# Row norms and down-weight sums moved from GpSimd to VectorE and spread over the loop, with another order of row blocks and loads

## The chip, the cores and the metric

The kernel runs on one core of a Trainium2 chip. The metric is the device time of one execution in microseconds (us), taken as the median of several runs. A core has five engines, each with its own queue of instructions: TensorE (PE, matrix products), VectorE (DVE), ScalarE (ACT), GpSimd (POOL) and SyncE (SP), which here issues most of the DMAs. An engine works through its queue in order, and a wait for a semaphore holds everything behind it.

## What is computed

```python
def reference(A_x, A_k_cache, A_v_cache, A_wq, A_wo, B_x, B_W_gate, B_W_up, B_W_down):
    x = A_x                                   # 1 x 2048 x 512, bfloat16
    xn = _layernorm(x, axis=-1)
    s = _A_ref(xn, A_k_cache, A_v_cache, A_wq, A_wo)   # q = xn @ wq, 32 heads of 128,
                                              # softmax(q k^T / sqrt(128)) v over 2048 keys, @ wo
    g = _silu(_B_ref(xn, B_W_gate, B_W_up, B_W_down))  # (relu(xn Wg) * (xn Wu)) @ Wd, F = 1792
    return x + s * g
```

## The kernel before, in words

The 2048 rows are worked in four row blocks of 512 (Q = 0 to 3), each of four tiles of 128 rows (n = 4Q to 4Q+3). The 32 heads are in eight groups of four. The main loop runs over 1024 *positions*: a block of the loop is one head with one row block, and has eight positions; each position makes the scores of 256 keys (`emit_S_tile`, L1481, three positions ahead), the exponential on ACT (L1493) and the product with V (`emit_PV_tile`, L1590). At the end of a block `emit_norm_block` divides by the row sums on DVE (L1510, L1513) and turns the result by DMA on SP's queue (L1518). The first eight blocks alternate between heads 0 and 1 (`hq_of`), so that a row block is used twice before the next is needed.

All other work is put at positions by hand, at the end of the function: `put(P, ...)` places products on PE, `aside(P, ...)` places work of the other engines at position P of the first blocks. What is placed at a position is issued after its scores and ahead of its product with V. What bears on the change:

- The layer norm. `front` makes the first four row tiles one by one ahead of the loop: statistics and aggregate on DVE (L398, L404), a square root on ACT (L407), the reciprocal on DVE, the norm itself on DVE for tile 0 and on POOL for tiles 1 to 3 (`ln_norm`, L431), a transpose on PE. PE then projects four heads of row block 0 (`head_q`, L503), whose results go out of PSUM by `q_out` (L513 on ACT, L515 on DVE). Row blocks 1, 2, 3 follow in `front`: four statistics, four aggregates and a chain of twelve small DVE instructions for the reciprocal square root (`ln_coef`, L419 to L425), then four norms on POOL, then four DMA transposes on SP into `xnT` (`ln_rows_turn`, L449; for block 3 at position 8).
- The plain projections, `emit_qplain` (L758): a head's queries of one row block from `xnT`, placed at positions 8, 10, 20, 24 and later.
- `emit_tx` (L581 to L589): four DVE sums over row blocks 0 and 2, later over 1 and 3, which the gated products need. Products are made in Strassen's manner: seven products (m = 1 to 7) of sums of blocks in place of eight.
- The gated unit, `emit_gu` (from GU0 = position 13, a step at each position; from GU1 = 67 for the other two row blocks). The 1792 columns are worked in chunks of 128, two chunks in seven steps, each step with two products (`gu_prod`, L1037) in one pair of PSUM banks. `gu_out` takes each to SBUF, most on DVE (a copy L1051, sums L1052), one on ACT (L1060). A product of the next step may add into a bank that this step's DVE instruction has to copy first. The lower rows' multiply is on POOL (L1073), the upper rows' on DVE (`gu_hi`, L1081), issued in the step of its product m = 3.
- `gu_prep`: a chunk's weights W are scaled (L605 on ACT; for chunks 0 and 1 L607 on POOL) and four sums SG made on POOL (L612 to L617).
- The down product (`emit_d`, L1129): its weight is loaded at position 20 (L651), scaled on DVE at 25 and 28 (L657), and its four sums of 128x1792 are made on POOL at positions 30, 36, 42, 48 (`emit_wd_sums`, L668 to L674). `emit_hs` makes sums of the gated unit's result on DVE. `emit_sw` scales a part of Wq on POOL (L635) and makes four sums there.

## Time and profile before

| | |
|---|---|
| median of 3 runs | 1301.07 us (1300.12 to 1302.04) |
| the profiled execution | 1303.03 us, its span 1301.6 us |
| PE busy | 1250.4 us (96%) |
| ACT busy | 1049.4 us (81%) |
| DVE busy | 929.2 us (71%) |
| POOL busy | 778.6 us (60%) |
| mean granted clock of TensorE | 0.990 |

In a row of the timeline stand the start and the duration in us, the engine, the line, the operation, out<-in, size and count, and in brackets how long the engine was idle ahead of it and what ended that. A row of groups has `xcount | busy, mean ns | idle before`. A row of a stretch has the time of each engine in it, then the granted clock, the DMA's share and GB/s.

### The profile page before, as it was taken

What the parts mean: (1) busy time and instruction counts of PE and PEld (TensorE: products, weight loads), DVE (VectorE), ACT (ScalarE), POOL (GpSimd) and SP (SyncE); (2) the same over time, 40 slices, a digit from 0 to 9 for tenths busy, and PEclk for the clock granted to TensorE, in tenths of its full rate; (3) what the DMA queues carried; (4) which work ended last, traced back from release to release, by engine and by line L of the source; (5) the groups of instructions that cost most, each with busy time, mean ns of one, the idle gap of its engine ahead of it and who ended that gap; (6) DMA issues with size and microseconds to landing.
All of it is one profiled execution on the core that took longest, in us unless ns stands there. A gap on an engine that the chain in (4) does not pass through costs nothing.

```text
span 1301.6 us, 29330 instructions
## 1 busy us (share of the span) xinstructions
PE 1250.4 (96%) x11957; PEld 819.3 (63%) x11957; DVE 929.2 (71%) x1389; ACT 1049.4 (81%) x1114; POOL 778.6 (60%) x879
## 2 busy tenths in 40 slices
...
GB/s 186 49 106 38 72 47 33 82 38 42 116 56 50 50 62 66 50 50 65 58 45 40 56 58 55 50 46 74 58 49 50 66 65 47 50 66 111 134 34 134
DMA packets 287396, 84.73 MB, mean 65 GB/s; under 512 B 265504, under 2 KB 287264, under 8 KB 287264
## 3 DMA queue, kind: packets, MB, share of 16 engines
...
## 4 chain that ended last, share of the span: by engine, by line
PE 80%; DVE 3%; issue 1%; ACT 0%; DVEq 0%; ACTq 0%
PE ps_acc L1590 33%; PE ps_r L1481 31%; PE ps_r L920 5%; PE ps_r L1320 3%; PE ps_r L1380 2%; PE ps_r L1037 2%; PE ps_r L1129 2%; PE ps_r L1622 1%; PE ps_r L787 1%; DVE g_sb L1159 1%; PE ps_r L1411 1%; PE ps_r L1412 0%; DVE uB L1052 0%; ACT PT L1493 0%; PE ps_r L1703 0%
## 5 line engine op out<-in xcount | busy, mean ns | idle before, releaser
L1493 ACT ACTIVATE PT<-ps_r 128x1024 bf16<-128x1024 f32 x1024 | 993.3, 1028 | 211.9 <-PE ps_r L1481 200.3
L1590 PEld LDWEIGHTS ps_acc<-V_sb,PT 128*128 128x128 bf16 x8192 | 544.3, 98 | 238.2 <-issue 36.8
L1590 PE MATMUL ps_acc<-V_sb,PT 128*128 128x129 bf16 x8192 | 629.1, 221 | 4.4 <-DVE Onorm L1513 3.4
L1481 PE MATMUL ps_r<-QT_sb,KT_sb 128*128 128x512 bf16 x2048 | 601.5, 381 | 9.8 <-ACT PT L1493 3.0
L925 DVE TENSOR_TENSOR UVR<-UVR,ps_r 128x512 f32<-128x512 f32 (+1 forms) x228 | 168.7, 755 | 85.2 <-PE ps_r L920 83.1
L1481 PEld LDWEIGHTS ps_r<-QT_sb,KT_sb 128*128 128x128 bf16 x2048 | 159.9, 98 | 37.4 <-DVE UVR L925 4.3
L1290 DVE TENSOR_TENSOR s_acc<-s_acc,ps_r 128x1024 f32<-128x1024 f32 x130 | 156.8, 1219 | 32.6 <-PE ps_r L1320 22.5
L885 POOL TENSOR_TENSOR TI<-xn_sb 128x512 f16<-128x512 f16 x48 | 55.9, 1165 | 96.8 <-PE ps_r L920 96.8
L1298 DVE TENSOR_TENSOR s_acc<-s_acc,ps_r 128x512 f32<-128x512 f32 x116 | 77.4, 686 | 22.1 <-PE ps_r L1380 17.9
L1513 DVE TENSOR_TENSOR Onorm<-ps_acc,rz_sb 128x512 bf16<-128x512 f32 x127 | 87.8, 692 | 4.4
L925 DVE TENSOR_TENSOR QT_sb<-UVR,ps_r 128x512 bf16<-128x512 f32 x72 | 49.5, 688 | 52.8 <-PE ps_r L920 50.4
L1073 POOL TENSOR_TENSOR hT<-gA,uA 128x512 f16<-128x512 bf16 x28 | 36.3, 1298 | 77.7 <-DVE uA L1052 51.7
L1510 DVE RECIPROCAL rz_sb<-ps_acc 128x4 f32<-128x4 f32 x127 | 23.0, 181 | 75.2 <-PE ps_acc L1590 74.6
L1348 POOL TENSOR_TENSOR TI<-OX 128x512 f16<-128x512 f16 x28 | 32.0, 1166 | 65.1 <-issue 65.1
L885 POOL TENSOR_TENSOR TI<-xnT 128x512 f16<-128x512 bf16 x36 | 41.6, 1156 | 39.4 <-PE ps_r L920 21.1
L1052 DVE TENSOR_TENSOR c<-c,ps_r 128x512 f32<-128x512 f32 x56 | 38.5, 687 | 28.1 <-PE ps_r L1037 26.5
L1236 POOL TENSOR_TENSOR WX<-Wo_sb 128x512 f16<-128x512 bf16 x7 | 8.1, 1156 | 83.0 <-DVE Wo_sb L1226 83.0
L1037 PE MATMUL ps_r<-xn_sb,SG 128*128 128x512 f16 x168 | 49.6, 391 | 6.7 <-POOL SG L617 5.4
L885 POOL TENSOR_TENSOR TI<-xn_sb,TI 128x512 f16<-128x512 f16 x48 | 55.9, 1165 | 0.0
L993 POOL TENSOR_TENSOR QT_sb<-UVR,UVR 128x512 bf16<-128x512 f32 x24 | 29.8, 1275 | 39.9 <-DVE UVR L925 39.9
L920 PE MATMUL ps_r<-TI,SI 128*128 128x512 f16 x126 | 47.8, 379 | 0.0
L1037 PE MATMUL ps_r<-xnT,W 128*128 128x512 bf16 x112 | 34.7, 393 | 13.5 <-DVE c L1051 6.9
...
## 6 DMA issues: line engine op xcount, KB each, us to landing
...
```

Source lines behind the costliest of these rows:

```text
L885: return sem_ui.sig(pool.tensor_tensor(dst, x, y, o))
L920: return sem_up.sig(pe.matmul(dst, lhs, rhs, start=start, stop=stop, skip_group_check=True))
L925: dve.tensor_tensor(dst, x, ps, ALU.add))
L1037: ins = pe.matmul(ps_r[:, bank, :], L(i), R(i), start=(i == 0 and m in (1, 6, 7)), stop=(i == HC - 1 and m in (2, 3, 4)), skip_group_check ...
L1052: dve.tensor_tensor(dst[:], a[:], ps, ALU.add))
L1290: t = sem_opa.sig(dve.tensor_tensor(dst, dst, sb, op))
L1298: t = dve.tensor_tensor(dst, dst, sb, op)
L1320: ins = pe.matmul(ps_r[:, bank, :], o_b(g, j, i, e), o_a(g, j, i, r), start=(i == 0), stop=(i == GH - 1))
L1481: ins = pe.matmul(ps_r[:, 2 * s + tt, :], KT_sb[h % 2][:, t * 128:(t + 1) * 128], QT_sb[qt_slot[(h, Q)]][:], start=True, stop=True)
L1493: act.activation(PT[pb][:], ps_r[:, 2 * s:2 * s + 2, :], ACTF.Exp, scale=scale / WSC)
L1513: dve.tensor_tensor(Onorm[ob][:], o_ap, rz_sb[:].to_broadcast([128, 4, Dh]), ALU.mult))
L1590: ins = pe.matmul(o_ap, PT[pb][:, tt, j * 128:(j + 1) * 128], V_sb[vb][:, t, 0:VW], start=(t == 0 and j % 2 == 0), stop=(t == KT - 1 and j ...
```

## The change

1. **Norms on DVE.** `ln_norm` runs on DVE for all tiles. `ln_rows` and its kin are replaced by pieces (`ln_piece`: "s" statistics, "c" coefficients, "n" norms, "t" turns). For tiles 0 to 3, the statistics of the next tile stand ahead of each norm, and PE transposes tile 1 ahead of the first projection.
2. **Row block 2 is second.** `LQ = (0, 2, 1, 3)` is the order of row blocks in the first eight blocks of the loop. Block 2 is normed in `front`; blocks 1 and 3 share one chain at position 14, with norms at 15 to 18 and turns at 16 and 18. Of the first four query evictions ACT now makes the first and the third.
3. **Scales.** Chunks 0 and 1 and the part of Wq are scaled on DVE. The sums stay on POOL.
4. **Down-weight sums** are on DVE, each in two pieces (four and three chunks), from position 32 to 49.
5. **Upper rows' multiply**: `gu_hi` is issued a step later, behind that step's `gu_out`; a chunk's later `gu_prep` a step earlier.
6. **Loads**: ACT's queue issues row block 2 and the first V, SP's both parts of Wq and chunk 0 ahead of row block 1, then the second K and V, chunk 1, block 3, chunk 2.
7. **Places**: the gated unit begins at 12 and 66; the down product, its HS sums and the row sums move with it (each one position earlier, the second `emit_tx` from 17 to 27).

The names of L429 and above move by some lines: L431 is L436 afterwards, L607 is L625, L1037 is L1056, L1051 and L1052 are L1070 and L1071, L1081 is L1100, L449 is L453.

```diff
-issue_wq(1, act)
+issue_wq(1)
+load_xq(2, act)
 issue_kt(0)
+issue_v(0, act)
+gu_load(0)
 load_xq(1)
-issue_v(0)
-load_xq(2)
 issue_kt(1)
 issue_v(1)
+gu_load(1)
 load_xq(3)
-for c in range(NW):
-    gu_load(c)
+gu_load(2)
...
+LQ = (0, 2, 1, 3)
+
+def li(n):
+    return 4 * LQ.index(n // 4) + n % 4
...
-    if ns[0] < 4:
-        _wait(act, atok)
-        tok = sem_sq.sig(act.activation(sqv[:, a:b_, :], mv[:, a:b_, 1:2], ACTF.Sqrt, bias=eps_sb[:]))
-        _wait(dve, tok)
-        return sem_ln3.sig(dve.reciprocal(rstd[:, a:b_, :], sqv[:, a:b_, :]))
...
-def ln_norm(eng, sem, n, ctok):
-    _wait(eng, ctok)
-    return sem.sig(
-        eng.tensor_scalar(xrow(n), x_sb[:, n, :], mv[:, n, 0:1], rstd[:, n, 0:1],
-                          op0=ALU.subtract, op1=ALU.mult))
-
+ln_tok = {}
 xt_ready = {Q: [] for Q in range(QB)}
 nm_tok = {}
 
-def ln_rows(Q):
-    ns = list(range(4 * Q, 4 * Q + 4))
-    return ln_coef(ns, [ln_stats(n) for n in ns][-1])
-
-def ln_rows_norm(Q, ctok):
-    for n in range(4 * Q, 4 * Q + 4):
-        nm_tok[n] = ln_norm(pool, sem_nm, n, ctok)
-
-def ln_rows_turn(Q):
-    for n in range(4 * Q, 4 * Q + 4):
-        _wait(sp, nm_tok[n])
-        xt_tok = sem_xq[Q].sig(
-            sp.dma_start_transpose(xnT[:, :, n * 128:(n + 1) * 128], xrow(n)))
-    xt_ready[Q] = [xt_tok]
-
-def head_norm(n):
-    ctok = ln_coef([n], ln_stats(n))
-    eng, sem = (dve, sem_ln4) if n == 0 else (pool, sem_nm)
-    return ln_norm(eng, sem, n, ctok)
+def ln_norm(n, ctok):
+    _wait(dve, ctok)
+    nm_tok[n] = sem_nm.sig(
+        dve.tensor_scalar(xrow(n), x_sb[:, n, :], mv[:, li(n), 0:1], rstd[:, li(n), 0:1],
+                          op0=ALU.subtract, op1=ALU.mult))
+    return nm_tok[n]
+
+def ln_piece(kind, ns):
+    if kind == "s":
+        for n in ns:
+            ln_tok["s"] = ln_stats(n)
+    elif kind == "c":
+        ln_tok["c"] = ln_coef(ns, ln_tok["s"])
+    elif kind == "n":
+        for n in ns:
+            ln_norm(n, ln_tok["c"])
+    else:
+        for n in ns:
+            _wait(sp, nm_tok[n])
+            xt_tok = sem_xq[n // 4].sig(
+                sp.dma_start_transpose(xnT[:, :, n * 128:(n + 1) * 128], xrow(n)))
+        if n % 4 == 3:
+            xt_ready[n // 4] = [xt_tok]
...
+def head_aggr(n, stok):
+    _wait(dve, stok)
+    return sem_ln2.sig(dve.bn_aggr(mv[:, n, :], stats[:, n, :]))
+
+def head_sqrt(n, atok):
+    _wait(act, atok)
+    return sem_sq.sig(act.activation(sqv[:, n, :], mv[:, n, 1:2], ACTF.Sqrt, bias=eps_sb[:]))
+
+def head_norm(n, qtok):
+    _wait(dve, qtok)
+    return ln_norm(n, sem_ln3.sig(dve.reciprocal(rstd[:, n, :], sqv[:, n, :])))
...
     toks = {0: q_out(act, 0, 0, ps_r[:, 0, :], p[0])}
-    stok = [ln_stats(4), ln_stats(5)][-1]
+    ln_piece("s", rows(2)[:2])
     toks[1] = q_out(dve, 1, 0, ps_r[:, 1, :], p[1])
     ring_tok[0] = [toks[0], toks[1]]
-    stok = [ln_stats(6), ln_stats(7)][-1]
-    for h in (2, 3):
-        toks[h] = q_out(dve, h, 0, ps_r[:, h, :], p[h])
+    toks[2] = q_out(act, 2, 0, ps_r[:, 2, :], p[2])
+    toks[3] = q_out(dve, 3, 0, ps_r[:, 3, :], p[3])
     ring_tok[1] = [toks[2], toks[3]]
-    ctok = ln_coef(list(range(4, 8)), stok)
-    ln_rows_norm(1, ctok)
-    ln_rows_turn(1)
-    for Q in (2, 3):
-        ctok = ln_rows(Q)
-        if Q == 3:
-            gu_prep(0, pool)
-        ln_rows_norm(Q, ctok)
-        if Q == 2:
-            ln_rows_turn(2)
-    gu_prep(1, pool)
+    ln_piece("s", rows(2)[2:])
+    ln_piece("c", rows(2))
+    ln_piece("n", rows(2))
+    ln_piece("t", rows(2))
+    gu_prep(0, dve)
+    ln_piece("s", rows(1))
+    gu_prep(1, dve)
...
-        gu_tok[(c, "s")] = sem_sg.sig(pool.tensor_scalar(wflat, wflat, GSC, None, op0=ALU.mult))
+        gu_tok[(c, "s")] = sem_uw.sig(dve.tensor_scalar(wflat, wflat, GSC, None, op0=ALU.mult))
     _wait(pool, gu_tok[(c, "s")])
...
-        k = sem_sw.sig(pool.tensor_scalar(wflat, wflat, WSC, None, op0=ALU.mult))
+        _wait(dve, wq_tok(pr))
+        if pr == 1:
+            _wait(dve, qpl_tok[1])
+        k = sem_uw.sig(dve.tensor_scalar(wflat, wflat, WSC, None, op0=ALU.mult))
...
-def emit_wd_sums(k):
+def emit_wd_sums(k, part):
     DH = D // 2
-    b11, b12 = Wd_sb[:, 0:HF, 0:DH], Wd_sb[:, 0:HF, DH:D]
-    b21, b22 = Wd_sb[:, HF:FC, 0:DH], Wd_sb[:, HF:FC, DH:D]
+    i0, i1 = (0, 4) if part == 0 else (4, HF)
+    W1, W2_ = Wd_sb[:, i0:i1], Wd_sb[:, HF + i0:HF + i1]
+    T = [WdT[:, j, i0:i1] for j in range(3)]
+    b11, b12, b21, b22 = W1[:, :, 0:DH], W1[:, :, DH:D], W2_[:, :, 0:DH], W2_[:, :, DH:D]
     if k == 0:
-        _wait_all(pool, [wd_tok[0], wd_tok[1], sem_nm.cur()])
-    elif k != 2:
-        _wait(pool, wd_tok["k"])
-    if k == 0:
-        t = pool.tensor_tensor(WdT[:, 0], b12, b11, ALU.subtract)
+        _wait_all(dve, [wd_tok[0], wd_tok[1]])
+        t = dve.tensor_tensor(T[0], b12, b11, ALU.subtract)
     elif k == 1:
-        t = pool.tensor_tensor(WdT[:, 1], b22, WdT[:, 0], ALU.subtract)
+        _wait(dve, wd_tok[("k", part, 0)])
+        t = dve.tensor_tensor(T[1], b22, T[0], ALU.subtract)
     elif k == 2:
-        t = pool.tensor_tensor(Wd16[:, 0:HF, DH:D], b22, b12, ALU.subtract)
+        t = dve.tensor_tensor(Wd16[:, i0:i1, DH:D], b22, b12, ALU.subtract)
     else:
-        t = pool.tensor_tensor(WdT[:, 2], WdT[:, 1], b21, ALU.subtract)
-    t = sem_wdt.sig(t)
-    if k != 2:
-        wd_tok["k"] = t
-    wd_tok["t"] = t
+        _wait(dve, wd_tok[("k", part, 1)])
+        t = dve.tensor_tensor(T[2], T[1], b21, ALU.subtract)
+    wd_tok[("k", part, k)] = wd_tok["t"] = sem_wdt.sig(t)
...
-        return b % 2, b // 2
+        return b % 2, LQ[b // 2]
...
-        if m == 3:
-            hi_c = c
-    if any(m == 3 for _, m, _k in st):
-        gu_hi(hi_c)
+    for c in gu_open:
+        gu_hi(c)
+    gu_open[:] = [c for c, m, _k in st if m == 3]
     for c, m, k in st:
         if m == 4 and c + NW < NCH:
             gu_load(c + NW)
-            gu_later.append((n + 4, c + NW))
+            gu_later.append((n + 3, c + NW))
     if gu_later and n >= gu_later[0][0]:
         gu_prep(gu_later.pop(0)[1])
     if n == 4:
         gu_prep(2)
+    if n % (len(gu_steps) // 2) == len(gu_steps) // 2 - 1:
+        for c in gu_open:
+            gu_hi(c)
+        gu_open.clear()
...
-GU0, GU1 = 13, 67
+GU0, GU1 = 12, 66
...
-for P, h, Q in ((8, 0, 1), (10, 1, 1), (20, 0, 2), (24, 1, 2), (30, 0, 3), (34, 1, 3), (38, 2, 2), (42, 3, 2)):
+for P, h, Q in ((9, 0, 2), (11, 1, 2), (21, 0, 1), (25, 1, 1), (30, 0, 3), (34, 1, 3), (38, 2, 2), (42, 3, 2)):
     put(P, (emit_qplain, 1, h, Q))
...
-aside(8, ln_rows_turn, 3)
 for k in range(4):
-    aside(10 + k // 2, emit_tx, 0, k)
-    aside(17 + k, emit_tx, 1, k)
-    aside(30 + 6 * k, emit_wd_sums, k)
+    aside(9 + k // 2, emit_tx, 0, k)
+    aside(27 + k, emit_tx, 1, k)
+    aside(32 + 5 * k, emit_wd_sums, k, 0)
+    aside(34 + 5 * k, emit_wd_sums, k, 1)
+aside(12, ln_piece, "s", rows(3)[:2])
+aside(13, ln_piece, "s", rows(3)[2:])
+aside(14, ln_piece, "c", rows(1, 3))
+aside(15, ln_piece, "n", rows(1)[:2])
+aside(16, ln_piece, "n", rows(1)[2:])
+aside(16, ln_piece, "t", rows(1))
+aside(17, ln_piece, "n", rows(3)[:2])
+aside(18, ln_piece, "n", rows(3)[2:])
+aside(18, ln_piece, "t", rows(3))
```

POOL's queue from the last constant on; W_57, W_58, W_59 are the weights of chunks 0, 1, 2, SG_77 and on their sums. Before:

```order
L297 MEMSET V_sb 128x16 x2
L431 TENSOR_SCALAR xn_sb<-x_sb_55,mv_59,rstd_60 128x512 x11
L607 TENSOR_SCALAR W_57_74<-W_57_74 128x1024
L612 TENSOR_TENSOR SG_77<-W_57_74 128x256
L613 TENSOR_TENSOR SG_77<-W_57_74 128x256
L615 TENSOR_TENSOR SG_77<-SG_77,W_57_74 128x256
L617 TENSOR_TENSOR SG_77<-W_57_74,SG_77 128x256
L431 TENSOR_SCALAR xn_sb<-x_sb_55,mv_59,rstd_60 128x512 x4
L607 TENSOR_SCALAR W_58_75<-W_58_75 128x1024
L612 TENSOR_TENSOR SG_78<-W_58_75 128x256
L613 TENSOR_TENSOR SG_78<-W_58_75 128x256
```

After:

```order
L296 MEMSET V_sb 128x16 x2
L630 TENSOR_TENSOR SG_77<-W_57_74 128x256
L631 TENSOR_TENSOR SG_77<-W_57_74 128x256
L633 TENSOR_TENSOR SG_77<-SG_77,W_57_74 128x256
L635 TENSOR_TENSOR SG_77<-W_57_74,SG_77 128x256
L630 TENSOR_TENSOR SG_78<-W_58_75 128x256
L631 TENSOR_TENSOR SG_78<-W_58_75 128x256
L633 TENSOR_TENSOR SG_78<-SG_78,W_58_75 128x256
L635 TENSOR_TENSOR SG_78<-W_58_75,SG_78 128x256
L1092 TENSOR_TENSOR hT_51<-gA_86,uA_83 128x512
```

The fifteen norms and the two scales are gone from POOL, and the first chunk's sums are its first work.

DVE around the gated steps 2 to 4 (c_63 is the copy of product 1, c_64 and c_65 sums with it, hT_52 the upper rows' result). Before:

```order
L1052 TENSOR_TENSOR gB_88<-c_63_80,ps_r 128x512
L1052 TENSOR_TENSOR uB_85<-c_65_82,ps_r 128x512
L1081 SCALAR_TENSOR_TENSOR hT_52<-gB_88,uB_85 128x512
L1510 RECIPROCAL rz_sb_64<-ps_acc 128x4
L1513 TENSOR_TENSOR Onorm_66<-ps_acc,rz_sb_64 128x512
L1051 COPY c_63_80<-ps_r 128x512
L1052 TENSOR_TENSOR uA_83<-c_64_81,ps_r 128x512
L1052 TENSOR_TENSOR c_64_81<-c_63_80,ps_r 128x512
L581 TENSOR_TENSOR xn_sb<-xnT 128x1024
L1052 TENSOR_TENSOR c_65_82<-c_63_80,ps_r 128x512
```

After, behind the four statistics of block 3, eight aggregates and most of the chain, which stand among and ahead of these steps:

```order
L425 SCALAR_TENSOR_TENSOR nwt_62<-nwt_62,sqv_61 128x8
L426 SCALAR_TENSOR_TENSOR rstd_60<-nwt_62,rstd_60 128x8
L1070 COPY c_63_80<-ps_r 128x512
L1071 TENSOR_TENSOR uA_83<-c_64_81,ps_r 128x512
L1100 SCALAR_TENSOR_TENSOR hT_52<-gB_88,uB_85 128x512
L436 TENSOR_SCALAR xn_sb<-x_sb_55,mv_59,rstd_60 128x512 x2
L1533 RECIPROCAL rz_sb_64<-ps_acc 128x4
L1536 TENSOR_TENSOR Onorm_66<-ps_acc,rz_sb_64 128x512
L1071 TENSOR_TENSOR c_64_81<-c_63_80,ps_r 128x512
L436 TENSOR_SCALAR xn_sb<-x_sb_55,mv_59,rstd_60 128x512 x2
L1071 TENSOR_TENSOR c_65_82<-c_63_80,ps_r 128x512
L1071 TENSOR_TENSOR uB_85<-c_65_82,ps_r 128x512
```

The end of the chain of blocks 1 and 3 stands ahead of step 3's copy, the upper rows' multiply stands behind the copy and the sum of its step, and norms stand in pairs behind steps 3 and 4.

SP's queue from the first turns on (Onorm is a block's result of attention, Wd_sb the down weight). Before:

```order
L449 DMA_TRANSPOSE xnT<-xn_sb 128x4x128 x8
L1518 DMA_TRANSPOSE OT_store_65<-Onorm_66 128x4x128
L449 DMA_TRANSPOSE xnT<-xn_sb 128x4x128 x4
L1518 DMA_TRANSPOSE OT_store_65<-Onorm_66 128x4x128
L369 DMA W_57_74<-in_B_W_gate_dram 128x4x128
L369 DMA W_57_74<-in_B_W_up_dram 128x4x128
L369 DMA W_58_75<-in_B_W_gate_dram 128x4x128
L369 DMA W_58_75<-in_B_W_up_dram 128x4x128
L651 DMA Wd_sb_53<-in_B_W_down_dram 128x14x512
L369 DMA W_59_76<-in_B_W_gate_dram 128x4x128
L369 DMA W_59_76<-in_B_W_up_dram 128x4x128
```

After:

```order
L453 DMA_TRANSPOSE xnT<-xn_sb 128x4x128 x4
L1541 DMA_TRANSPOSE OT_store_65<-Onorm_66 128x4x128
L368 DMA W_57_74<-in_B_W_gate_dram 128x4x128
L368 DMA W_57_74<-in_B_W_up_dram 128x4x128
L1541 DMA_TRANSPOSE OT_store_65<-Onorm_66 128x4x128
L453 DMA_TRANSPOSE xnT<-xn_sb 128x4x128 x4
L368 DMA W_58_75<-in_B_W_gate_dram 128x4x128
L368 DMA W_58_75<-in_B_W_up_dram 128x4x128
L453 DMA_TRANSPOSE xnT<-xn_sb 128x4x128 x4
L672 DMA Wd_sb_53<-in_B_W_down_dram 128x14x512
L368 DMA W_59_76<-in_B_W_gate_dram 128x4x128
L368 DMA W_59_76<-in_B_W_up_dram 128x4x128
```

Eight of the twelve turns now stand behind the first two blocks' results, four of them behind chunk 4's load, and the down weight's load follows them.

57 lines of the change are left out of this document (34 added, 23 removed).

## The prediction

> **What bounds the kernel now.** First the table by stage (us, then the busy time of each engine, PEclk the granted clock).
>
> ```profile
> 30.00:60.00 30.00, 18.79 (x116) 10.05 (x117) 15.27 (x34) 8.59 (x10) 29.44 (x19) 0.83 0.26 53
> 60.00:100.00 40.00, 38.05 (x281) 19.48 (x279) 35.15 (x51) 27.68 (x31) 26.51 (x30) 1.00 0.36 97
> 100.00:160.00 60.00, 49.29 (x333) 25.22 (x332) 46.49 (x65) 31.58 (x35) 41.31 (x40) 0.94 0.27 51
> 160.00:345.00 185.00, 171.16 (x1406) 108.70 (x1405) 146.69 (x225) 106.17 (x123) 80.53 (x91) 0.99 0.24 50
> 345.00:1301.00 956.00, 952.10 (x9638) 640.33 (x9636) 666.87 (x956) 857.21 (x892) 585.48 (x686) 1.00 0.34 64
> ```
>
> From 345 us on PE is busy 952.1 of 956 us, so whatever is gained ahead of that reaches the end undiminished. The losses lie ahead: 11.2 us idle in 30 to 60, where POOL is busy 29.4 of 30 us, and 10.7 us in 100 to 160. The timeline of PE names the waits.
>
> ```profile
> 32.56 1.87 PE L758 MATMUL ps_r<-xnT,Wq_sb 128*128 128x512 bf16 x4 [5.41 <-DMA xnT<-xn_sb]
> 41.18 0.59 PE L1037 MATMUL ps_r<-xnT,W 128*128 128x512 bf16 x2 [0.75 <-POOL W L607]
> 45.17 0.61 PE L1037 MATMUL ps_r<-xn_sb,SG 128*128 128x512 f16 x2 [3.40 <-POOL SG L617]
> 56.28 1.04 PE L1037 MATMUL ps_r<-xnT,W 128*128 128x512 bf16 x2 [4.44 <-POOL W L607]
> 105.72 0.61 PE L1037 MATMUL ps_r<-xnT,W 128*128 128x512 bf16 x2 [1.88 <-DVE c L1051]
> 123.87 0.60 PE L1037 MATMUL ps_r<-xnT,W 128*128 128x512 bf16 x2 [1.59 <-DVE c L1051]
> 132.84 0.60 PE L1037 MATMUL ps_r<-xn_sb,SG 128*128 128x512 f16 x2 [1.96 <-POOL SG L617]
> 142.05 0.60 PE L1481 MATMUL ps_r<-QT_sb,KT_sb 128*128 128x512 bf16 x2 [1.97 <-DVE cuv L792]
> ```
>
> The first four have one root: POOL makes the row norms at 2.07 us each, and the scales and sums of the first two chunks stand behind them. The other four stand beside long POOL instructions. The rows of both, from the groups and the timeline:
>
> ```profile
> L431 POOL TENSOR_SCALAR xn_sb<-x_sb,mv,rstd x15: 2066/2073/2085, 6.8 to 51.3; 128x512 bf16<-128x512 bf16 x15
> L431 DVE TENSOR_SCALAR xn_sb<-x_sb,mv,rstd x1: 413/413/413, 4.7 to 4.7; 128x512 bf16<-128x512 bf16 x1
> 100.93 3.58 POOL L670 TENSOR_TENSOR WdT<-Wd_sb,WdT 128x1792 f16<-128x1792 bf16 x1
> 102.13 2.94 DVE L1081 SCALAR_TENSOR_TENSOR hT<-gB,uB 128x512 f16<-128x512 bf16 x1
> L1081 DVE SCALAR_TENSOR_TENSOR hT<-gB,uB x28: 677/691/2935, 51.9 to 301.8; 128x512 f16<-128x512 bf16 x28
> ```
>
> The upper rows' multiply, 0.69 us as a rule, took 2.94 us and ended at 105.07, beside POOL's sum that ended at 104.51; the copy that PE needed stood behind it on DVE. So the POOL sums cost PE nothing directly: they hold up DVE.
>
> **What the change takes away.** Norms on DVE are 0.41 us instead of 2.07, and POOL holds neither norms nor scales ahead of the first chunk. The four waits go: 5.41 + 0.75 + 3.40 + 4.44 = 14.0 us. The clock of 0.83 over those 30 us is 30 x 0.17 = 5.1 us of lost work; it follows these waits, and I count it whole. The down-weight sums on DVE, in eight pieces, take away the four waits of 100 to 160: 1.88 + 1.59 + 1.96 + 1.97 = 7.4 us (the third was POOL's own lateness; the Wq scale ahead of it moves to DVE too). The clock there, 0.94, is 60 x 0.06 = 3.6 us; I take half, 1.8, since the last of that stage's stalls, among the HS sums, remain. In the head, two of four query evictions move to ACT:
>
> ```profile
> 19.03 0.82 PE L1481 MATMUL ps_r<-QT_sb,KT_sb 128*128 128x512 bf16 x3 [1.66 <-DVE QT_sb L515]
> 19.67 9.28 ACT L1493 ACTIVATE PT<-ps_r 128x1024 bf16<-128x1024 f32 x10 [0.76 <-PE ps_r L1481]
> ```
>
> PE's 1.66 us wait goes, but ACT is what paces here (0.93 us for each position), and it sat idle 0.76: 0.8 us. For the new order of loads and the first four norms I take 0, between 1.5 better (no row waits for POOL) and 3 worse (ACT now issues two 512 KB loads ahead of its first square root). The upper multiply, a step later, lets the copy that starts the next chunk go ahead of it; 1.0 us over 160 to 345, between 0 and 3. Together 14.0 + 5.1 + 7.4 + 1.8 + 0.8 + 1.0 = 30.1 us.
>
> **What it costs.** The prices:
>
> ```profile
> 27.45 2.47 DVE L398 BATCH_NORM_STATS2 stats<-x_sb 128x6 f32<-128x512 bf16 x4
> 29.95 0.38 DVE L404 BATCH_NORM_AGGREGATE mv<-stats 128x2 f32<-128x6 f32 x4
> 31.39 0.16 DVE L424 SCALAR_TENSOR_TENSOR nwt<-nwt,sqv 128x4 f32<-128x4 f32 x1
> 31.59 0.16 DVE L425 SCALAR_TENSOR_TENSOR rstd<-nwt,rstd 128x4 f32<-128x4 f32 x1
> 114.29 0.69 DVE L1081 SCALAR_TENSOR_TENSOR hT<-gB,uB 128x512 f16<-128x512 bf16 x1
> 114.89 0.69 DVE L1051 COPY c<-ps_r 128x512 f32<-128x512 f32 x1
> 119.48 0.62 PE L1590 MATMUL ps_acc<-V_sb,PT 128*128 128x129 bf16 x8
> 121.23 0.62 PE L1590 MATMUL ps_acc<-V_sb,PT 128*128 128x129 bf16 x8
> L581 DVE TENSOR_TENSOR xn_sb<-xnT 128x1024 f16<-128x1024 bf16 x2 | 1.4, 688 | 2.2 <-DMA xnT<-xn_sb 2.2
> ```
>
> A position with a gated step is 1.75 us on PE (119.48 to 121.23). DVE instructions that wait for nothing start 0.60 us apart (114.29 to 114.89), those of the coefficient chain 0.20 (31.39 to 31.59).
>
> *The second block's turn.*
>
> ```profile
> L449 SPq DMA_TRANSPOSE xnT<-xn_sb x12: 1189/1190/1292, 23.8 to 53.4; - x12
> DMA to landing us min/median/max: 2.4/2.4/4.0
> ```
>
> The first turn started at 23.8, behind a norm of 2.07: the coefficients were done near 21.7. With one eviction less on DVE they are done at 21.0, the first norm at 21.45, and SP turns a row every 1.19 us. The last is issued at 25.1 and landed at 27.5. PE stood ready at 32.56 - 5.41 = 27.15 in position 8; position 9 comes 0.93 later and 0.8 earlier, 27.3. I take 0.5 us, between 0 and 2.5.
>
> *The burst at positions 12 to 18.* Over the first seven gated steps DVE has its own 14 instructions (14 x 0.60 = 8.4), the statistics (2.5), eight aggregates and twelve chain steps (0.75 + 12 x 0.20), eight norms (8 x 0.41 = 3.3) and a normalisation (a 512-column instruction on PSUM as the copy, 0.60, and a small one, 0.20): 18.2 us beside 7 x 1.75 = 12.25 on PE. Of the excess of 6.0, DVE may still lag by 1.3 when PE goes on: 4.6 us, between 2 and 7. What PE meets first is the piece of 3.2 us at position 14: the copy of step 3 stands behind it, and step 4 waits for that copy, about 2.6 us (3.2 and the copy's 0.6, less 1.2 until PE asks for it).
>
> *The down weight's load.* It is issued at position 20, and SP now has the turns of two row blocks ahead of it.
>
> ```profile
> 58.20 0.37 SPq L369 DMA_DIRECT2D W<-in_B_W_gate_dram  x1
> 58.61 0.51 SPq L369 DMA_DIRECT2D W<-in_B_W_up_dram  x1
> L651 SPq DMA_DIRECT2D Wd_sb<-in_B_W_down_dram x1: 507/507/507, 65.2 to 65.2; - x1
> DMA to landing us min/median/max: 9.1/9.1/9.1
> 79.47 1.09 DVE L657 TENSOR_SCALAR Wd_sb<-Wd_sb 128x3584 bf16<-128x3584 bf16 x1
> ```
>
> Before, it landed at 74.3, 5 us ahead of its use. Now, from block 1's normalisation in position 15: 9 x 1.19 for the turns and 0.88 for a chunk's loads, 11.6, and 9.1 to land: 20.7 us. DVE comes to the scale in position 25, after ten positions and two projections, each 0.87 by columns (2048 of a step's 4104): 10 x 1.75 + 1.7 = 19.2. DVE waits some 1.5 us there, with every gated copy behind it; between 0 (if PE stalls in between anyway) and 4.5.
>
> *The sums.* Eight pieces of at most 0.69 us, as L581 with its 1024 columns, at positions 32 to 49. DVE's own work in a step is 1.20 and 0.1 for normalisation, so 0.45 is free, and a piece oversteps by about 0.2: 2 us with the Wq scale, between 0 and 5.
>
> *The clock.* A stall of 1.88 us at 105 was followed by a stretch of lower clock, one of 1.59 at 123 by none:
>
> ```profile
> 100.00:120.00 20.00, 17.73 (x121) 9.34 (x120) 14.28 (x21) 10.96 (x12) 13.07 (x14) 0.91 0.15 33
> 120.00:140.00 20.00, 16.38 (x122) 8.61 (x119) 15.87 (x20) 11.24 (x13) 19.68 (x17) 1.00 0.15 34
> ```
>
> The burst's longest stall, about 2.6 us, is of the first kind: 20 x 0.09 = 1.8 us once, between 0 and 3.6. [...]
>
> Costs: 0.5 + 4.6 + 1.5 + 2.0 + 1.8 = 10.4. The gain is 30.1 - 10.4 = 19.7 us. The profiled execution, 1303.03 us (span 1301.6), becomes 1283.3; it lies 1.96 above the median of 1301.07, so the median becomes **1281.4**. The costs at their upper ends are 22.6 and the loads 3 more: the gain falls to 4.5; at their lower ends it is over 30.
>
> **Rivals.** *DVE and POOL in each other's way (slower).* Place: positions 9 to 61. There DVE has 8 sums for the row transforms, 8 norms, 14 upper multiplies, 8 down-weight sums, 3 scales and 4 HS sums, 45 instructions that read and write SBUF alone. That POOL can hold such ones up, the 2.94 us show, and in a milder form the mean of this group of the row transforms, 1.39, against 0.69 for L581 above, of the same size:
>
> ```profile
> L586 DVE TENSOR_TENSOR xn_sb<-xnT,xn_sb 128x1024 f16<-128x1024 bf16 x2 | 2.8, 1394 | 0.0
> ```
>
> DVE is at 88% already in 60 to 100; some 4 us of room would be left in the stage. Slower needs a mean wait of (19.7 + 4) / 45 = 0.53 us; at 0.8 each it is 36 - 4 - 19.7 = 12 us slower, 1313. Against it: POOL's long pieces, the sums of 3.58 and the norms of 2.07, all go. Chance 0.04. At half that wait, 0.4 each, 14 us of the gain go: 1295; 0.06. [...]
>
> *The queue decides.* The down weight lands 4.5 us late, the next chunk's weights behind it, ACT waits for these with the exponentials behind, and a second stretch of low clock follows: 3.0 + 1.8 + some 4 from the loads in the head: 1289 to 1293. For it: SP's issues at 2 to 11 us were held up (5.42 us for K). Chance 0.14.
>
> ```profile
> 2.11 5.42 SPq L314 DMA_TRANSPOSE KT_sb<-in_A_k_cache_dram  x1
> ```
>
> *DVE keeps pace.* The bursts fit into PE's other waits, costs of 3 instead of 10.4: 1274. Chance 0.07.
>
> *It doesn't do what it says.* The second block's turn stays late (its load, now on ACT's queue, comes no earlier), the first stall is moved, not removed, and the burst eats the rest: within 0.2%, about 2.6 us, which is what a measurement of this kernel can tell from no change. Chance 0.03.
>
> **How the numbers follow.** The forecast, 1275 to 1289, has 0.66. The range takes in the queue's case and the edge of the fast one: 1273 to 1293. Faster: 0.66 + 0.14 + 0.07 + 0.06 = 0.93; same 0.03; slower 0.04.
>
> **What would show it.** Right: the stall ahead of the first plain projection under 2.5 us; the first gated step near 33 us instead of 41 to 45; no wait of PE on POOL in 30 to 60; all upper multiplies at 0.7 to 1.0 us; a PE wait of 2 to 3 us on the copy some 6 us after the first gated step. The step on the down weight is right if DVE's first scale of it waits for a DMA. It would be wrong if DVE's SBUF instructions average over 1.2 us in 30 to 130, or if PE's stalls after 60 us add up to more than before.

## The result and the profile after

The changed kernel takes **1281.8 us** (median of 4 runs, 1281.09 to 1283.86) against 1301.55 before (4 runs): a ratio of 0.9851, 95% interval 0.9834 to 0.9868, so 19.75 us less. Its profiled execution took 1281.32 us, with a span of 1279.8 and a mean granted clock of 0.992.

The stages first, with the columns as before (length, then busy time of PE, PEld, DVE, ACT and POOL, the granted clock, DMA share, GB/s).

```profile
30.00:60.00 30.00, 23.70 (x161) 12.38 (x162) 26.36 (x59) 16.55 (x18) 8.22 (x11) 0.89 0.27 53
60.00:100.00 40.00, 37.74 (x276) 19.68 (x277) 37.72 (x56) 25.94 (x29) 23.45 (x26) 1.00 0.40 99
100.00:160.00 60.00, 53.58 (x409) 32.09 (x416) 49.46 (x77) 33.87 (x38) 33.50 (x39) 0.97 0.32 69
160.00:345.00 185.00, 172.53 (x1443) 111.35 (x1466) 146.92 (x233) 114.65 (x131) 70.94 (x82) 0.99 0.26 57
```

In 30 to 60 us POOL falls from 29.4 to 8.2 us, DVE rises to 26.4, and PE does 23.7 us of work instead of 18.8. DVE, not POOL, is now the engine next to PE. What PE still waits for from 28 us on, in its timeline:

```profile
28.25 0.81 PE L777 MATMUL ps_r<-xnT,Wq_sb 128*128 128x512 bf16 x3 [0.46 <-ACT PT L1516]
32.63 0.59 PE L1056 MATMUL ps_r<-xnT,W 128*128 128x512 bf16 x2
...
42.66 0.60 PE L1056 MATMUL ps_r<-xnT,W 128*128 128x512 bf16 x2 [2.21 <-DVE c L1070]
...
46.70 1.02 PE L1613 MATMUL ps_acc<-V_sb,PT 128*128 128x129 bf16 x8 [2.76 <-DVE Onorm L1536]
...
77.70 0.61 PE L1056 MATMUL ps_r<-xnT,W 128*128 128x512 bf16 x2 [0.99 <-DVE c L1070]
...
119.65 1.02 PE L1613 MATMUL ps_acc<-V_sb,PT 128*128 128x129 bf16 x8 [2.25 <-DVE Onorm L1536]
...
294.39 0.59 PE L1613 MATMUL ps_acc<-V_sb,PT 128*128 128x129 bf16 x4 [3.29 <-DVE Onorm L1536]
```

The first plain projection waits 0.46 us instead of 5.41, the first gated step starts at 32.63, and no wait names POOL any more. The largest waits are of a kind that was no longer than 1.36 us before (from 20 to 345 us): PE's next product with V waits for DVE to normalise the block just finished (L1536). DVE's own timeline ahead of the wait that ends at 46.70 shows why:

```profile
41.91 0.69 DVE L1070 COPY c<-ps_r 128x512 f32<-128x512 f32 x1
42.52 0.68 DVE L1071 TENSOR_TENSOR uA<-c,ps_r 128x512 bf16<-128x512 f32 x1
43.12 0.68 DVE L1100 SCALAR_TENSOR_TENSOR hT<-gB,uB 128x512 f16<-128x512 bf16 x1
43.72 2.02 DVE L436 TENSOR_SCALAR xn_sb<-x_sb,mv,rstd 128x512 bf16<-128x512 bf16 x2
45.66 0.17 DVE L1533 RECIPROCAL rz_sb<-ps_acc 128x4 f32<-128x4 f32 x1
45.86 0.69 DVE L1536 TENSOR_TENSOR Onorm<-ps_acc,rz_sb 128x512 bf16<-128x512 f32 x1
```

Position 15 is the last of a block. Its extra work, two norms of 2.02 us together, is issued ahead of the block's normalisation, and PE's queue stands at the next product until that is done. The waits that end at 119.65 and 294.39 have the same form. Ahead of the first stands a piece of the down-weight sums at position 47 (1.15 us on DVE from 117.54). Ahead of the second stand three HS sums, which the change moved from position 120, the first of a block, to 119, the last of the block before:

```profile
291.29 0.68 DVE L712 TENSOR_TENSOR HS_sb<-hT 128x1024 f16<-128x1024 f16 x1
292.01 0.69 DVE L715 TENSOR_TENSOR hT<-hT 128x1024 f16<-128x1024 f16 x1
292.73 0.69 DVE L718 TENSOR_TENSOR HS_sb<-hT 128x1024 f16<-128x1024 f16 x1
```

Where the time came from is seen best by counting positions. The table gives the start of the n-th of the 1024 exponentials in ACT's timeline (n counts from 0 and runs three ahead of the loop's position):

| exponential | before, us | after, us | gained |
|---|---|---|---|
| 10 | 26.9 | 25.5 | 1.4 |
| 12 | 36.3 | 28.1 | 8.2 |
| 20 | 59.8 | 48.6 | 11.2 |
| 28 | 77.6 | 66.1 | 11.5 |
| 65 | 167.3 | 150.0 | 17.3 |
| 80 | 218.8 | 198.4 | 20.3 |
| 140 | 347.3 | 325.3 | 22.0 |
| 1020 | 1283.3 | 1261.4 | 22.0 |

From 140 on not a tenth is gained or lost in 900 us: what is gained ahead reaches the end.

### The profile page after: what moved, and what is told of

It reads as the page before. It is cut to its first block, busy times and chain, and to the rows that moved or that the text cites. A ratio compares the mean times of both kernels' runs of the same rounds, so it can differ in the third digit from the quotient of the medians.

```text
span 1279.8 us, 29110 instructions
## 1 busy us (share of the span) xinstructions
PE 1231.3 (96%) x11745; PEld 818.3 (64%) x11957; DVE 928.8 (73%) x1403; ACT 1048.1 (82%) x1115; POOL 726.2 (57%) x856
## 3 DMA queue, kind: packets, MB, share of 16 engines
q8 instruction: 95, 1.56, 0.5%
## 4 chain that ended last, share of the span: by engine, by line
PE 88%; DVE 8%; issue 3%; DMA 1%; ACT 0%; SPq 0%; DVEq 0%
PE ps_acc L1613 35%; PE ps_r L1504 32%; PE ps_r L939 5%; PE ps_r L1056 4%; PE ps_r L1152 3%; PE ps_r L1343 3%; PE ps_r L1403 2%; PE ps_r L806 1%; DVE c L1071 1%; PE ps_r L1645 1%; DVE hT L1100 1%; DVE uA L1071 1%; DVE Onorm L1536 1%; DVE c L1070 1%; DMA Wq_sb<-in_A_wq_dram 1%
## 5 line engine op out<-in xcount | busy, mean ns | idle before, releaser
L1504 PE MATMUL ps_r<-QT_sb,KT_sb 128*128 128x512 bf16 x1849 | 557.2, 380 | 14.6 <-DVE QT_sb L811 1.9
L1536 DVE TENSOR_TENSOR Onorm<-ps_acc,rz_sb 128x512 bf16<-128x512 f32 x127 | 87.8, 691 | 4.4
L630 POOL TENSOR_TENSOR SG<-W 128x256 f16<-128x256 bf16 x28 | 20.1, 719 | 64.2 <-ACT W L623 42.8
L1056 PE MATMUL ps_r<-xn_sb,SG 128*128 128x512 f16 x168 | 49.1, 389 | 1.1 <-DVE c L1071 0.9
L1071 DVE TENSOR_TENSOR c<-c,ps_r 128x512 f32<-128x512 f32 x56 | 38.2, 682 | 9.6 <-PE ps_r L1056 7.8
```

The costliest lines, as they stand in the source:

```text
L1056: ins = pe.matmul(ps_r[:, bank, :], L(i), R(i), start=(i == 0 and m in (1, 6, 7)), stop=(i == HC - 1 and m in (2, 3, 4)), skip_group_check ...
L1071: dve.tensor_tensor(dst[:], a[:], ps, ALU.add))
L1504: ins = pe.matmul(ps_r[:, 2 * s + tt, :], KT_sb[h % 2][:, t * 128:(t + 1) * 128], QT_sb[qt_slot[(h, Q)]][:], start=True, stop=True)
L1536: dve.tensor_tensor(Onorm[ob][:], o_ap, rz_sb[:].to_broadcast([128, 4, Dh]), ALU.mult))
```

## The experiments

All times below are medians. The kernel before, run beside them, took 1301.36 us with the first four, 1301.01 with the next four and 1300.56 with the last four; ratios are to it. The changed kernel was not run again beside them: a difference from its 1281.8 us is one between sessions, on at least two chips, and the kernel before differs by up to 1.0 us between these.

**One part undone at a time.** First the down-weight sums, back on POOL:

```diff
-aside(32 + 5 * k, emit_wd_sums, k, 0)
-aside(34 + 5 * k, emit_wd_sums, k, 1)
+aside(30 + 6 * k, emit_wd_sums, k)
...
-t = dve.tensor_tensor(T[0], b12, b11, ALU.subtract)
+t = pool.tensor_tensor(WdT[:, 0], b12, b11, ALU.subtract)
...
```

> The changed kernel with the down-weight sums back on POOL, whole, at positions 30, 36, 42 and 48; all else stays. Theory (the sums hold up VectorE when POOL makes them): the waits of 100 to 160 us come back, 7.4 us and 1.8 of clock, less the 2.0 that the pieces cost on DVE: 7 us slower, 1286 to 1292, with upper multiplies of 2 to 3 us beside POOL pieces of 3.58 us. [...]

Measured: 1288.9 us, 0.9908 (0.9891 to 0.9924), 7.1 slower than the changed kernel. Two DVE rows, and the two POOL rows beside them:

```profile
81.01 3.96 DVE L607 TENSOR_TENSOR xn_sb<-xnT,xn_sb 128x1024 f16<-128x1024 bf16 x1
...
112.16 3.78 DVE L656 TENSOR_SCALAR Wq_sb<-Wq_sb 128x1024 bf16<-128x1024 bf16 x1
```

```profile
80.87 3.56 POOL L689 TENSOR_TENSOR WdT<-Wd_sb 128x1792 f16<-128x1792 bf16 x1
...
111.65 4.01 POOL L693 TENSOR_TENSOR Wd<-Wd_sb 128x1792 f16<-128x1792 bf16 x1
```

A row sum of 0.68 us takes 3.96 and a scale of 0.4 us takes 3.78; both end some 0.3 to 0.5 us after POOL's piece. PE waits 3.17 and 3.38 us behind them. The time is as the theory said, though it isn't the upper multiply that is caught this time, but the DVE instruction that starts beside POOL's piece and reads and writes SBUF alone. Beside the other two pieces (99.59 and 125.89 us) DVE has only instructions with an operand in PSUM, and those of 512 columns keep their 0.68 to 0.69 us. Why the one kind is held up and the other isn't, these rows don't show.

Second, the upper multiply back in its own step:

```diff
-for c in gu_open:
-    gu_hi(c)
-gu_open[:] = [c for c, m, _k in st if m == 3]
+for c, m, _k in st:
+    if m == 3:
+        gu_hi(c)
...
```

> The changed kernel with the upper rows' multiply back in its own step. Theory: 1.0 us slower (0 to 3), spread over 160 to 345 us as waits of PE on the copy that starts the next chunk. Rival: a multiply that is a step later stands ahead of a normalisation instead, for which PE also waits (2.25 us at 119); then undoing it makes no difference or up to 2 us faster, and the waits on the normalisation shrink.

Measured: 1288.73 us, 0.9901 (0.9885 to 0.9918), 6.9 slower. Neither the 1.0 of the theory nor the rival: two waits on the normalisation do shrink (2.76 to 1.71, 2.25 to 0.93), but a third grows from 0.70 to 2.24, and those on the copy grow by more. Between the two traces lie 9.1 us at exponential 140 (the trace here is of the slowest of the four runs, 1290.68 us). Of these, 5.9 are lost by exponential 60, where the theory expected none. DVE's timeline at one of the places:

```profile
76.27 0.69 DVE L1100 SCALAR_TENSOR_TENSOR hT<-gB,uB 128x512 f16<-128x512 bf16 x1
76.88 1.16 DVE L601 TENSOR_TENSOR xn_sb<-xnT 128x1024 f16<-128x1024 bf16 x1
77.96 1.55 DVE L678 TENSOR_SCALAR Wd_sb<-Wd_sb 128x3584 bf16<-128x3584 bf16 x1
79.43 0.68 DVE L1070 COPY c<-ps_r 128x512 f32<-128x512 f32 x1
```

The multiply stands in the one queue with the extra pieces, and the copy that starts a chunk stands behind all three: PE waits 2.19 us there, against 0.99 for the same copy (77.70) in the changed kernel, where the multiply comes after it. So most of what the later multiply brings, it brings early, by making room where DVE carries extra work. The other 3.2 us of the trace are lost between exponentials 60 and 140, where the theory had placed its loss: PE waits 1.07 us on the copy at 199.28, and a second window of half clock stands at 304.

Both edits together, as in the two diffs above, tell whether the two are one effect.

> The changed kernel with both undone: the down-weight sums whole on POOL and the upper multiply in its own step. Each of the two undone alone cost 7 us. If each term stands alone, as the sum took it: 14 us slower than the changed kernel, 1296. If the two are one effect (the pieces fit on DVE only with the later multiply, and that is worth something only because the pieces are there): 7 to 8 us, 1289. Between these, by the 4.1 us that the sums brought alone in the kernel before: 11 us, 1293; this is my guess.

| | multiply a step later | multiply in its own step |
|---|---|---|
| sums on DVE | 1281.8 | 1288.7 |
| sums on POOL | 1288.9 | 1288.4 |

1288.37 us, 0.9897 (0.9882 to 0.9912): 6.6 slower than the changed kernel, no more than each alone. My guess of 11 was wrong; in this kernel the two bring 6.6 us together and nothing apart. The sum had 7.4 + 1.8 - 2.0 for the one and 1.0 for the other, 8.2 in all: about right as a total, wrong as two terms.

Third, the loads in the old order.

```diff
-issue_wq(1)
-load_xq(2, act)
+issue_wq(1, act)
 issue_kt(0)
-issue_v(0, act)
-gu_load(0)
 load_xq(1)
+issue_v(0)
+load_xq(2)
 issue_kt(1)
 issue_v(1)
-gu_load(1)
 load_xq(3)
-gu_load(2)
+for c in range(NW):
+    gu_load(c)
```

> The changed kernel with the loads at the start in the old order (all of the gated chunks last, the second-used row block after the second's K and V). Theory: the loads are worth nothing by themselves, 0 (1.5 faster to 3 slower); the time up to position 10 stays within 1.5 us. Rival: the early load of the second-used row block and of chunk 0 is what lets the first plain projection and the first gated step start without a wait; then a wait of 3 us or more comes back ahead of one of them, and the time is 4 us slower or more.

Measured: 1282.1 us, 0.985 (0.9836 to 0.9865): the same. The loads brought nothing, as the sum had it; the rival falls.

Fourth, half of the norms back on POOL.

```diff
-nm_tok[n] = sem_nm.sig(dve.tensor_scalar(...))
+eng, sem = (pool, sem_ln4) if n // 4 in (1, 3) else (dve, sem_nm)
+nm_tok[n] = sem.sig(eng.tensor_scalar(...))
...
```

> The changed kernel with the norms of two of four row blocks (positions 15 to 18) back on POOL; the head's and the second-used block's stay on DVE. Theory: the burst on DVE loses 3.3 us of 18.2 and the waits of 2.21 and 2.76 us at 42 and 46 us shrink by 2 to 3 us with the clock behind them, but eight norms at 2.07 us are 16.6 us on POOL ahead of the sums of chunks 2 and 3: PE waits there 4 to 8 us. Net 3 us slower (1 faster to 6 slower). Rival: these norms are not needed soon, POOL (busy 8.2 of 30 us there) has room, and the kernel is 3 to 5 us faster.

Measured: 1291.62 us, 0.9923 (0.9908 to 0.9937), 9.8 slower, three times the theory. PE's waits on POOL's sums stay small (0.45 and 0.70 us). What I had left out stands on SP and DVE:

```profile
57.62 11.18 SPq L455 DMA_TRANSPOSE xnT<-xn_sb  x4
68.84 0.58 SPq L674 DMA_DIRECT2D Wd_sb<-in_B_W_down_dram  x1
```

```profile
76.80 1.09 DVE L680 TENSOR_SCALAR Wd_sb<-Wd_sb 128x3584 bf16<-128x3584 bf16 x1 [7.82 <-DMA Wd_sb<-in_B_W_down_dram]
```

The turns wait for POOL's norms on SP, the down weight's load is queued behind the turns and goes out at 68.84, and DVE stands 7.82 us at its first scale, with the copy behind it: PE waits 6.79 us. A projection's wait of 2.46 us on a turn (57.77) comes on top. This is the beginning of the prediction's rival "the queue decides", brought about by an edit that was meant for something else.

**One part alone, in the kernel before.** The sums in eight pieces on DVE, nothing else:

```diff
-aside(30 + 6 * k, emit_wd_sums, k)
+aside(33 + 5 * k, emit_wd_sums, k, 0)
+aside(35 + 5 * k, emit_wd_sums, k, 1)
...
```

> The kernel before with one part alone: the down-weight sums on DVE in eight pieces, at positions 33 to 50; norms, loads, order and the multiply's step stay as before. Theory of the sum (each term stands alone): 7.4 + 1.8 - 2.0, 7 us faster than before, 1294. Theory formed on the run with the multiply in its own step (the pieces find room on DVE only because the multiply goes a step later): of these 7 us some 6 are lost again as waits on the copy that starts a chunk, so 1 us faster (3 faster to 2 slower), 1300.

Measured: 1296.95 us, 0.9965 (0.9952 to 0.9978): 4.1 faster, between the two. PE's waits of 1.88, 1.59, 1.96 and 1.97 us give way to shorter ones (0.94, 0.71, 0.83, 0.47). In the traces the gain between exponentials 28 and 60 is 6.0 us, nearer to the sum's 7; 0.7 us were lost in the first 27 us, ahead of the edit's place. Why the pieces bring this there without the later multiply, and nothing in the changed kernel without it, I haven't settled. One difference is on record: here the pieces stand at 33 to 50, none at the last position of a block. In the changed kernel with the multiply in its own step, one stands with the multiply at position 39, ahead of the normalisation, and PE waits 2.24 us for that (105.95). No run shows whether that is all of it.

The norms and the first two scales on DVE, in the old order, three blocks in a row:

```diff
-nm_tok[n] = ln_norm(pool, sem_nm, n, ctok)
+nm_tok[n] = ln_norm(dve, sem_nm, n, ctok)
-gu_prep(0, pool)
+gu_prep(0, dve)
...
```

> The kernel before with one part alone: all norms and the scales of chunks 0 and 1 on DVE, in the old place and order (statistics, coefficients and norms of the three blocks in a row). Theory: most of the four waits of 30 to 60 us goes, since POOL's 2.07 us a norm are the root, but three blocks in a row are some 20 us of DVE, so the third block is turned near 37 us and the first projection's eviction waits: 8 us faster than before (4 to 11), 1293. Rival (spreading and order are what brings it): DVE's row of 20 us holds up evictions and normalisation as POOL's row did, and the time is within 3 us of before.

Measured: 1298.06 us, 0.9974 (0.9964 to 0.9983): 3.0 faster, as the rival said. PE's timeline, and DVE's ahead of it:

```profile
30.09 1.02 PE L757 MATMUL ps_r<-xnT,Wq_sb 128*128 128x512 bf16 x4 [1.56 <-DMA xnT<-xn_sb]
40.45 1.03 PE L1589 MATMUL ps_acc<-V_sb,PT 128*128 128x129 bf16 x8 [9.35 <-DVE Onorm L1512]
```

```profile
36.73 2.43 DVE L430 TENSOR_SCALAR xn_sb<-x_sb,mv,rstd 128x512 bf16<-128x512 bf16 x4
39.08 0.41 DVE L606 TENSOR_SCALAR W<-W 128x1024 bf16<-128x1024 bf16 x1
39.42 0.17 DVE L1509 RECIPROCAL rz_sb<-ps_acc 128x4 f32<-128x4 f32 x1
```

The wait of 5.41 us ahead of the first projection falls to 1.56, and one of 9.35 on the first block's normalisation takes its place: from 21 to 39 us DVE makes nothing but layer norm and the two scales. The faster engine alone is worth 3 us. The rest of the first 60 us comes with what else the change did there: the spreading, the order of the row blocks, the earlier gated unit, two evictions on ACT. No run takes these apart; that the spreading and the order bring most of it, since they let DVE's work interleave, is my reading.

**What POOL's work costs DVE.** POOL's multiply of the lower rows done twice, into the same tile:

```diff
-h_done[(Ql, k)] = h_done[(c, "lo")] = sem_hp.sig(pool.tensor_tensor(hT[0][:, k, :], g[:], u[:], ALU.mult))
+for _r in range(2):
+    h_done[(Ql, k)] = h_done[(c, "lo")] = sem_hp.sig(pool.tensor_tensor(hT[0][:, k, :], g[:], u[:], ALU.mult))
+    _wait(pool, h_done[(Ql, k)])
```

> The changed kernel with POOL's multiply of the lower rows done twice (the same product into the same tile, 28 more instructions of 1.33 us); DVE's and PE's work is unchanged. [...]

Measured: 1286.58 us, 0.9888 (0.9871 to 0.9906), 1286.49 to 1287.93 in three runs; a fourth, with the profile in it, took 3328.8 us, for no reason that I know, and is left out. So 4.8 us slower, at the upper end of my estimate: 2 us (0 to 5), from the 0.2 us that DVE's instructions which read and write SBUF alone wait on average in the changed kernel. For a trace there is one more run of it:

> The kernel with POOL's multiply of the lower rows done twice once more, for a trace of it (it was 5.5 us slower than the changed kernel). [...]

It took 1286.7 us. The groups of 28 to 175 us, first of the changed kernel, then of this one:

```profile
L1100 DVE SCALAR_TENSOR_TENSOR hT<-gB,uB 128x512 f16<-128x512 bf16 x14 | 11.4, 817 | 0.0
L436 DVE TENSOR_SCALAR xn_sb<-x_sb,mv,rstd 128x512 bf16<-128x512 bf16 x8 | 5.4, 710 | 0.0
...
L604 DVE TENSOR_TENSOR xn_sb<-xnT,xn_sb 128x1024 f16<-128x1024 bf16 x2 | 1.8, 916 | 0.0
L691 DVE TENSOR_TENSOR WdT<-Wd_sb,WdT 128x1024 f16<-128x1024 bf16 x1 | 1.7, 1668 | 0.0
```

```profile
L1102 DVE SCALAR_TENSOR_TENSOR hT<-gB,uB 128x512 f16<-128x512 bf16 x14 | 13.1, 938 | 0.0
L436 DVE TENSOR_SCALAR xn_sb<-x_sb,mv,rstd 128x512 bf16<-128x512 bf16 x8 | 6.2, 813 | 0.0
...
L604 DVE TENSOR_TENSOR xn_sb<-xnT,xn_sb 128x1024 f16<-128x1024 bf16 x2 | 2.3, 1158 | 0.0
...
L691 DVE TENSOR_TENSOR WdT<-Wd_sb,WdT 128x1024 f16<-128x1024 bf16 x1 | 1.7, 1668 | 0.0
```

The upper multiplies, the norms and the row sums grow by 0.10 to 0.24 us each, the pieces of the down-weight sums don't. The wait on the normalisation at 47 us goes from 2.76 to 3.21 and the one on the copy at 80 from 0.99 to 1.62, and PE waits nowhere on POOL. So the loss comes through DVE's longer instructions and not through POOL's own lateness, though the mean of the upper multiplies, 0.94 us against 0.82, stayed under the 1.0 that I had expected in that case.

**The place in DVE's queue.** The changed kernel, with the extra pieces of a block's last position issued behind its normalisation:

```diff
+own = side.pop((bq, pq), [])
+last = pq == NP - 1 and bq < GB
-for fn, *args in side.pop((bq, pq), []):
+for fn, *args in () if last else own:
     fn(*args)
...
 emit_PV_tile(gq, 1)
+for fn, *args in own if last else ():
+    fn(*args)
```

> The changed kernel with one thing moved: at the last position of each block (7, 15, 23, ...) DVE's extra pieces go behind the normalisation instead of ahead of it. Theory (the place in DVE's queue decides): the waits on the normalisation at 46.7, 119.7 and 294.4 us (2.76, 2.25, 3.29) and the stretches of half clock at 44.5, 119.6 and 293.7 (1.7 us of work each) shrink, and half of that comes back at the next copy: 6 us faster, 1276 (1272 to 1279). Rival (DVE's load decides, the waits only change their name): within 1.5 us of the changed kernel.

Measured: **1275.56 us**, 0.9802 (0.9787 to 0.9816), 6.2 faster than the changed kernel. The three waits in PE's timeline:

```profile
45.46 0.88 PE L1613 MATMUL ps_acc<-V_sb,PT 128*128 128x129 bf16 x8 [0.83 <-DVE Onorm L1536]
...
117.52 0.61 PE L1613 MATMUL ps_acc<-V_sb,PT 128*128 128x129 bf16 x8 [1.18 <-DVE Onorm L1536]
...
288.71 0.39 PE L1613 MATMUL ps_acc<-V_sb,PT 128*128 128x129 bf16 x4 [1.02 <-DVE Onorm L1536]
```

2.76, 2.25 and 3.29 became 0.83, 1.18 and 1.02, 5.3 us in all, and of the four windows of half clock (3.41 us each) between 20 and 345 us one is left. Part of that came back, as a wait of 1.21 us on ACT at 294.69 for one. No instruction was taken from DVE: the order in its queue decides, not its load.

On top of it, the burst lightened:

```diff
-aside(12, ln_piece, "s", rows(3)[:2])
-aside(13, ln_piece, "s", rows(3)[2:])
-aside(14, ln_piece, "c", rows(1, 3))
+aside(8, ln_piece, "s", rows(3))
+aside(12, ln_piece, "c", rows(1, 3))
...
```

> The kernel with the normalisation ahead of the extra pieces (1275.6 us), and besides it the statistics of the last row block at position 8, where DVE sat idle 2.9 us, and coefficients and norms one to two positions earlier. Theory (burst of 18.2 us on DVE against 12.25 on PE): 2.5 us leave the burst, the waits of 2.21 us on the copy and 0.83 on the normalisation go with the half clock behind them: 3 us faster than without it, 1273 (1271 to 1275). Rival (the same pieces now stand ahead of the row transforms and the first gated copies): no change, within 1 us.

Measured: 1275.66 us, 0.9802 (0.9787 to 0.9817): no change. The burst's wait of 2.21 us didn't go: it ends at 38.84 now, on a sum of an earlier gated step, behind the coefficients, as the rival said, and a window of half clock follows it as before. By the count of positions this kernel was still 2.0 us ahead from exponential 34 to 59; by 60 it was 0.8 ahead, and by 61 only 0.4. No wait had grown there. The stretches of 3.41 us around 134 us, first of this kernel, then of the one it builds on:

```profile
130.99:134.40 3.41, 1.19 (x8) 0.34 (x6) 3.34 (x7) 2.16 (x3) 0.95 (x2) 1.00 0.67 151
134.40:137.81 3.41, 3.19 (x15) 1.71 (x15) 1.58 (x3) 0.81 (x2) 2.58 (x4) 0.50 0.21 41
```

```profile
131.05:134.46 3.41, 2.57 (x22) 1.29 (x19) 3.41 (x6) 1.51 (x2) 2.90 (x4) 1.00 0.06 15
134.46:137.87 3.41, 2.02 (x16) 1.08 (x16) 3.34 (x7) 1.97 (x2) 1.23 (x2) 1.00 0.63 140
137.87:141.29 3.42, 3.42 (x29) 1.88 (x26) 2.61 (x5) 2.54 (x3) 2.84 (x4) 1.00 0.53 114
```

Both have the same two waits here, 0.84 and 1.38 or 1.39 us. In the first kernel both fall into one stretch, PE is busy 1.19 of 3.41 us, and the next stretch runs at half clock; in the second they fall into two, and the clock stays. So the rival had the time right and the place of the first wait; what took back the 2.0 us is the clock.

Last, on top of both, the output's multiplies behind the normalisation as well.

```diff
-for fn in later.pop(gq, []):
+due = later.pop(gq, [])
+for fn in () if last else due:
     fn()
...
+for fn in due if last else ():
+    fn()
```

> As the kernel with early statistics and the normalisation first, and also the output's multiplies (deferred pieces, two of 0.68 us) behind the normalisation at a block's last position. Theory: the waits of 1.51 us at 186 and 0.71 at 268 go: 1.5 us faster than without it, about 1271.5. Rival: they come back as waits on the products behind: within 0.5 us.

Measured: **1274.43 us**, 0.979 (0.9773 to 0.9807), the lowest median of all, 1.2 below the kernel that it builds on; the runs of the two overlap (1273.98 to 1276.13 against 1275.23 to 1276.9). The wait of 1.50 us at 186 fell to 0.30, and 0.75 came back on the next product; the wait of 0.71 at 268 stayed. By the count of positions nothing is gained between exponentials 65 and 1020 (0.30 us behind at both), which is what the rival said.

## Why the prediction was right, step by step

- **What bounds it, and that the gain reaches the end.** Right: 22.0 us at exponential 140, 22.0 at the last but three.
- **The four waits of 30 to 60 us and the clock there, with the burst against them.** The sum to 60 us was 14.0 + 5.1 + 0.8 - 0.5 - 4.6 - 1.8 = 13.0; measured at exponential 28, 11.5. All four went. That they go because the norms are on DVE was too short: alone, in the old order, that brings 3.0. The rest came with the other edits of this stretch, which no run takes apart.
- **The second block's turn** cost nothing that shows: the projection waits 0.46 us, for ACT. Just ahead of it PE waits 1.23 us (to 26.52) for the first block's normalisation, which stands behind statistics and a scale on DVE; the sum had no term for that.
- **The burst.** I had 4.6, of it 2.6 on the copy of step 3; the waits are 2.21 on that copy and 2.76 on the normalisation, 4.97 together. The size was right and the first wait too (it began 8 us after the first gated step, not 6); the second I had lumped into a lag. It was the one that could be had back: what stood at position 15 was ahead of a normalisation. The same holds for 3.29 us at 294, behind HS sums moved to position 119: the sum put that move at nothing.
- **The down weight's load.** I had 1.5; DVE came to the scale at 68.46, which is also when the load landed (issued at 60.56, 7.9 us): nothing. By the sign that I had named, a wait of DVE for the DMA, this step was not right. A tie, not cover: eight microseconds later on SP, it cost 6.8.

```profile
60.56 0.58 SPq L672 DMA_DIRECT2D Wd_sb<-in_B_W_down_dram  x1
```

```profile
67.85 0.69 DVE L530 TENSOR_SCALAR QT_sb<-ps_r 128x512 bf16<-128x512 f32 x1
68.46 1.63 DVE L678 TENSOR_SCALAR Wd_sb<-Wd_sb 128x3584 bf16<-128x3584 bf16 x1
```

- **The sums in pieces and the multiply's step.** These terms failed as terms. The pieces were to cost 2.0 (0 to 5): the waits while they run, from 85 to 125 us, are 0.70 + 0.38 + 2.25 = 3.3, with a window of half clock behind the last. The multiply was to bring 1.0 in 160 to 345: undone, it costs 6.9. Together they were to bring 8.2 and bring 6.6. The stalls among the HS sums, which I had said would remain, did remain: 0.75 + 0.60 + 1.24 = 2.6 us from 151 to 155 before, 0.84 + 1.38 = 2.2 at 137 to 139 now. Their half clock went, though, and by little: the window ahead was idle 1.89 us before and 1.82 now. That is luck.
- **The clock.** I counted 5.1 + 1.8 - 1.8 = 5.1 us. Between 20 and 345 us there were six windows of half clock and now there are four, two of them in a row behind the burst. PE was busy 19.6 us in the six and is 10.2 in the four; I take half of that as lost (in the trace before, four products of L758 take 1.87 us at 32.56, in such a window, and 1.03 at 116.87, at full clock), so 9.8 - 5.1 = 4.7 us came back. The sum was right, and the one window at 120 us replaces the one at 155.
- **The loads.** 0 predicted, 0.3 measured.
- **DVE and POOL in each other's way.** The rival needed 0.53 us on each of 45 instructions. Beyond the shortest of their kind in the traces (0.68, 0.41, 1.09 and 0.55 to 0.69 us) the upper multiplies wait 1.9 us in all, the norms 2.4, the pieces of the sums 2.7, the scales 1.5 and the row sums 0.5: 9 us, 0.2 each. The sign to look for, all upper multiplies at 0.7 to 1.0, held for the mean (0.82 up to 175 us) and not for all: seven of 28 are longer, up to 1.42. The sign against it, over 1.2 us for DVE's SBUF instructions of 30 to 130 us, did not appear: without the small coefficient steps they average 0.84. That 28 more POOL instructions cost 4.8 us shows that the rival was a real one with the wrong size.

PE's waits of 0.3 us and more from 60 to 345 us add up to 17.5 us, against 24.2 before, so the sign against the prediction did not appear. The median came out to 0.4 us, but by stage the sum was 1.5 too good ahead of 66 us and 3.8 too poor behind it (6.7 against 22.0 - 11.5 = 10.5). Behind 66 us the sums and the multiply brought no more than the sum had for them. But the run without both still gains 4.2 us on the kernel before between exponentials 28 and 140 (10.7 and 14.9 us ahead), where the rest of the sum was the load's minus 1.5. That comes from the other edits, which the sum put at nothing there and no run takes apart. What was left of the two errors, 2.0 us between the profiled executions (1283.3 forecast, 1281.32 measured), went with their distances to the medians. That the gain lies where I put it is shown; its closeness is partly luck.
